# A gated linear-attention and GEGLU kernel: a new written order, a new split of work among the engines, and state products over whole 128-column tiles

## The chip, the cores and the metric

The kernel runs on one core of a Trainium2 chip. The core has five engines, each with a queue that it works off in order: TensorE (PE, matrix products; its weight loads are shown apart as PEld), VectorE (DVE), ScalarE (ACT), GpSimd (POOL) and SyncE (SP, which here only issues DMAs). POOL issues DMAs too. PE writes to PSUM, which DVE and ACT read; the other tiles are in SBUF.

The metric is the time of one execution on the device in microseconds. Before the change the median of three runs is 279.8 us (279.54 to 279.91).

## The reference

What is computed is a recurrence with a complex decay per step, followed by a gated feed-forward layer on its output (4 batches, 8 heads, 768 steps, 48 wide; 3072 tokens of 384 in the second part):

```python
mag = np.sqrt(a_re * a_re + a_im * a_im)
scale = np.minimum(mag, 0.999) / (mag + 1e-06)
a_re_n, a_im_n = (a_re * scale, a_im * scale)
for t in range(S):
    new_re = ar * S_re - ai * S_im
    new_im = ar * S_im + ai * S_re
    S_re, S_im = (new_re + kv, new_im)
    y[:, :, t] = np.einsum('bhd,bhde->bhe', q[:, :, t], S_re)
...
g = x @ w_gate
gelu = 0.5 * g * (1.0 + erf(g * inv_sqrt2))
ffn_out = gelu * (x @ w_val) @ w_out
res_gate = 1.0 / (1.0 + np.exp(-(x @ w_res)))
return x + res_gate * ffn_out
```

## The kernel before

**Tiles.** The sequence of a batch is cut into three stretches of 256 steps, each of two chunks of 128. A pair p = 4s + b is stretch s of batch b, so there are twelve pairs, 0 to 11, and the names of steps carry it: `QR6` is a step of pair 6, `X6.1` one of its second chunk, `AT6.1.0` one of the first four heads of that chunk. The feed-forward layer runs in seven units: pair 0, pair 1, then 2 and 3, 4 and 5, 6 and 7, 8 and 9, 10 and 11. `GP3.0` is a step of unit 3.

**The chain of one pair.** Loads `Lar`, `Lai`, `Lk`, `Lq`, `Lvf` on SP, 192 KB each. The gates: squares `SQI`, `SQR` (ACT or DVE), their capped sum `ADD` (DVE), `LNR` and `EXR` (ACT, 1/|re|), the tangent `TH` (DVE), `LM` (ACT, log magnitude), `ATN` (ACT, phase), running sums over the chunk by a product with a triangular matrix, `CSL` for the magnitude and `CST` for the phase (PE, fp32), `EX` and `EI` (ACT, the exponential and its inverse), then `OFF`, `FR`, `ABS` (reduction of the phase), `SIN` and `COS` (ACT). Products: `KE`, `QE` scale k and q, and `KR`, `QR` turn them into `padK` and `padQ`, 96 of 128 columns wide, the other 32 being zero (DVE). Attention within the chunk: for pairs 0 to 4 `TP` and `CP` transpose through PE and copy back, from pair 5 on `QT` and `KT` are transposing DMAs on SP; then `AT` (PE), `AM` (mask, DVE), `Y` (PE), `X` (copy to bf16, ACT or DVE).

**What is carried on.** `DK` (PE, line 612) adds up the state of a chunk, `MI` and `ED` take it over (DVE). Between stretches the state is decayed by `EN` (line 619) with a factor that `MM` and `MN` multiply together (lines 472 and 475) from small values that go through DRAM (`DR`, `DS`, `DE`, `DI`, `DT` on POOL), and copied to bf16 by `EB`. The phase is carried from chunk to chunk by `CRA` and `CRB` (line 533), which scale the last rows of the phase tile, and a DMA `CDA` or `CDB` (POOL, line 538), which adds the last of them to the next chunk's first row ahead of its `CST`.

**A unit.** `XT` and `XC` transpose x through PE for pairs 0 to 4, `XD` by DMA from pair 5 on; `GP` and `VP` are the gate and value products (PE), twelve steps of 512 columns each (six double steps in the units of one pair, so that GP0.0 to GP0.5 are all), `GE` the gelu (ACT), `HM` its product with the value (DVE), `RP` and `SG` the residual gate (PE, ACT), `OP` the output product (PE), `OT` its gating (DVE), `RX` the addition of x (POOL or DVE, line 729), `ST` the store (SP). Weights come by POOL's DMAs `Wg`, `Wv`, `Wr`, `Wo`; `HOLDW` and `HOLDO` are one-element copies on POOL that wait for a load of a_im and so hold back the weight loads written behind them.

**What sets the order.** `ORDER` is one list of step names, worked off from front to back under a manual schedule; each engine gets its instructions in that order, and waits between engines follow from the data and from tiles that are used again. The words `log`, `trig` and `gelu` in it load one of three function tables on ACT. `PARAMS['eo']` names the engine of single steps; `on(name, default)` looks it up. The PSUM tiles of the sums, the gate and value products and the transposes share four banks.

Of the kernel before, what the change touches and what calls it, by code (L numbers as in the profile page):

```python
# [64 lines left out]
 'eo': {'CP0.0.0.0': 'DVE',  # L65
        'CP0.0.1.0': 'DVE',
        'CP0.1.0.0': 'DVE',
        'CP0.1.1.1': 'ACT',
        'CP1.0.0.1': 'ACT',
        'CP1.1.0.0': 'DVE',  # L70
        'CP1.1.0.1': 'ACT',
        'CP1.1.1.0': 'DVE',
        'CP2.0.1.0': 'DVE',
        'CP3.0.0.1': 'ACT',
        'CP3.0.1.0': 'DVE',
        'CP3.0.1.1': 'ACT',
# [749 lines left out]
```

## Time and profile before

| | us |
|---|---|
| median of three runs | 279.8 |
| the profiled execution's span | 277.7 |
| PE busy | 239.6 (86%) |
| DVE busy | 225.6 (81%) |
| ACT busy | 199.7 (72%) |
| POOL busy | 82.6 (30%) |
| ACT table loads | 21, 26.9 in all |

The busy time of an engine is the time in which at least one of its instructions runs; neighbouring instructions of one engine overlap at their ends, so a busy engine is not always a full one. The granted TensorE clock is a share of full speed. DMA engines moved 41.33 MB, 149 GB/s over the span. 163,200 packets of them came from SP's queue, 7,488 from POOL's.

### The profile page before, as it was taken

To read this page: it belongs to the slowest core of one execution; us is meant where nothing else is said; L and a number is where in the kernel's file an instruction comes from. 1 tells how busy PE (TensorE), PEld (TensorE's weight loads), DVE (VectorE), ACT (ScalarE), POOL (GpSimd) and SP (SyncE) were. 2 spreads that over 40 slices of the span, in tenths; PEclk is the share of its full clock that TensorE was granted. 3 is DMA by queue.
4 is the path that set the end of the run, shared out by engine and by line. 5 is a ranking of instruction groups with operands and counts; after the bars stand their busy time and mean duration, and the time that the engine had idled before them with its cause. 6 is when DMAs were issued, how large, how long until landed. Compare 5 with 4: busy or idle time off the path is not lost.

```text
span 277.7 us, 5218 instructions
## 1 busy us (share of the span) xinstructions
PE 239.6 (86%) x1854; PEld 145.5 (52%) x1854; DVE 225.6 (81%) x390; ACT 199.7 (72%) x346; POOL 82.6 (30%) x127
## 2 busy tenths in 40 slices
PE   0446477977999978999999999999999999999993
PEld 0114345754687654546755466555566445654451
DVE  1369866698899999899999999999979999743533
ACT  5558867799989988999978889894776834415410
POOL 4013160320360464242546522600717400010001
PEclk9999955999899997999999999999999999999999
DMA  7999999999980499859969996889995794221003
GB/s 147 205 192 187 191 184 184 183 183 207 205 169 0 74 195 176 148 67 223 193 131 207 191 204 148 133 175 211 163 189 138 137 221 87 62 74 56 0 0 113
DMA packets 170712, 41.33 MB, mean 149 GB/s; under 512 B 162624, under 2 KB 170688, under 8 KB 170688
## 3 DMA queue, kind: packets, MB, share of 16 engines
q1 hardware_dynamic: 163200, 37.04, 67.3%
q0 software_dynamic: 7488, 3.97, 11.5%
q8 instruction: 14, 0.23, 0.3%
q14 instruction: 10, 0.08, 0.1%
HBM read 31.33 MB, written 4.76 MB: 130 GB/s over the span
## 4 chain that ended last, share of the span: by engine, by line
PE 54%; ACT 15%; DVE 12%; issue 8%; DMA 7%; POOL 2%; SPq 0%; DVEq 0%; POOLq 0%; ACTq 0%
PE gv L692 23%; PE sums L717 13%; ACT ar L370 4%; PE sums L455 4%; PE sums L488 4%; DVE h L703 3%; PE sums L707 3%; PE at L604 2%; ACT m L370 2%; DMA QT<-padQ 2%; ACT CS L370 2%; DMA KT<-padK 2%; DVE atm L607 1%; ACT Ei L370 1%; ACT L793 1%
## 5 line engine op out<-in xcount | busy, mean ns | idle before, releaser
L370 ACT ACTIVATE h<-gv 128x512 bf16<-128x512 f32 x72 | 41.5, 598 | 29.2 <-PE gv L692 28.3
L703 DVE SCALAR_TENSOR_TENSOR h<-h,gv 128x512 bf16<-128x512 bf16 x72 | 47.0, 681 | 14.0 <-PE gv L692 13.7
L692 PE MATMUL gv<-xT,wg 128*128 128x512 bf16 (+1 forms) x252 | 55.9, 359 | 1.8 <-ACT xT L377 1.5
L692 PE MATMUL gv<-xT,wv 128*128 128x512 bf16 (+1 forms) x252 | 55.0, 356 | 0.6 <-DVE h L703 0.6
L717 PE MATMUL sums<-wo,h 128*128 128x384 bf16 x288 | 50.5, 330 | 0.0
L717 PEld LDWEIGHTS <-h 128*128 128x128 bf16 x288 | 27.8, 99 | 18.3 <-issue 1.7
L692 PEld LDWEIGHTS <-wg 128*128 128x128 bf16 x252 | 24.9, 101 | 22.6 <-issue 3.4
L692 PEld LDWEIGHTS <-wv 128*128 128x128 bf16 x252 | 24.7, 100 | 21.4 <-issue 1.6
L607 DVE TENSOR_TENSOR atm<-at,mask 128x512 bf16<-128x512 f32 x48 | 31.7, 682 | 3.9 <-PE at L604 3.6
L793 ACT ACT_TABLE_LOAD x21 | 26.9, 1283 | 1.1 <-PEq L810 0.7
L370 ACT ACTIVATE ar<-ar 128x768 f32<-128x768 f32 (+1 forms) x31 | 25.6, 841 | 1.1 <-DVE m L431 1.0
L729 POOL TENSOR_TENSOR ot<-ot,x 128x384 f32<-128x384 f32 x13 | 15.2, 1189 | 32.4 <-DVE ot L722 32.3
L722 DVE SCALAR_TENSOR_TENSOR ot<-sg,sums 128x384 f32<-128x384 f32 x24 | 13.2, 549 | 10.4 <-PE sums L717 10.0
L378 POOL CAST v<-vf 128x384 bf16<-128x384 f32 x14 | 8.6, 619 | 42.4 <-DMA vf<-in_v_dram 42.4
L443 POOL DMA_DIRECT2D m<-d x16 | 11.3, 705 | 33.5 <-DVE M L475 23.2
L455 PE MATMUL sums<-m,lt 128*128 128x384 f32 x24 | 11.9, 583 | 10.5 <-DVE lt L286 8.7
L538 POOL DMA_DIRECT2D ai<-G x16 | 13.1, 820 | 24.3 <-ACT ai L370 13.9
L488 PE MATMUL sums<-ai,ut 128*128 128x384 f32 x40 | 17.8, 545 | 2.2 <-issue 1.0
L370 ACT ACTIVATE sg<-sums 128x384 f32<-128x384 f32 x24 | 11.6, 493 | 9.5 <-PE sums L707 9.4
L707 PE MATMUL sums<-wr,xT 128*128 128x384 bf16 x72 | 15.7, 332 | 0.0
L651 PE MATMUL y<-v,atm 128*128 128x48 bf16 x192 | 13.2, 187 | 2.7 <-DVE atm L607 2.7
L469 POOL DMA_DIRECT2D m<-d x16 | 13.8, 897 | 5.3 <-DMA d<-Ei 5.3
(89 smaller groups left out, 451.2 us busy)
## 6 DMA issues: line engine op xcount, KB each, us to landing
ai<-in_a_im_dram SPq DMA_DIRECT2D x24, 192.0 KB, 3.8
ar<-in_a_re_dram SPq DMA_DIRECT2D x24, 192.0 KB, 3.9
k<-in_k_dram SPq DMA_DIRECT2D x24, 192.0 KB, 3.9
q<-in_q_dram SPq DMA_DIRECT2D x24, 192.0 KB, 4.4
vf<-in_v_dram SPq DMA_DIRECT2D x24, 192.0 KB, 4.1
out_dram<-ot SPq DMA_DIRECT2D x24, 192.0 KB, 2.5
wg<-in_moe_w_gate_dram POOLq DMA_DIRECT2D x4, 288.0 KB, 8.1
wv<-in_moe_w_val_dram POOLq DMA_DIRECT2D x4, 288.0 KB, 9.0
```

Of the source, the lines that this page charges most:

```text
L370: return nc.scalar.activation(out=out, in_=in_, func=func, **kw)
L455: st.add("CSL%d.%d" % (p, c), "PE", lambda c=c: nc.tensor.matmul(out=st["csl", (p, c)], lhsT=lmat[c], rhs=part(("m2", p), (c,)), start=Tru ...
L469: st.add("DT%d.%d" % (p, u), "POOL", lambda u=u: nc.gpsimd.dma_start(out=st["m3", p][u * D:(u + 1) * D].rearrange("p r h -> p (r h)"), in_ ...
L488: return r + [nc.tensor.matmul(out=o, lhsT=tmat[c if s == 0 else 1], rhs=part(("ai", p), (c,)), start=not both, stop=True)]
L607: st.add("AM" + sfx, "DVE", lambda: nc.vector.tensor_tensor(out=st["atm", i], in0=st["at", i], in1=mask4, op=OP.mult), r=[("at", i)], w=[( ...
L651: r.append(nc.tensor.matmul(out=ys, lhsT=st["atm", (p, c, hg)][:, j], rhs=st["v", p][:, c, h], start=True, stop=first))
L692: st.add("%sP%d.%d" % (nm.upper(), u, f), "PE", lambda f=f, fs=fs, nm=nm, w=w: [nc.tensor.matmul(out=st[nm + "p", (u, f)][:, j * 256:j * 2 ...
L703: st.add("HM%d.%d" % (u, f), "DVE", lambda f=f, h2=h2: nc.vector.scalar_tensor_tensor(out=h2(), in0=h2(), scalar=0.5, in1=gv(("vp", (u, f) ...
L707: st.add("RP%d.%d" % (u, jj), "PE", lambda jj=jj: [nc.tensor.matmul(out=st["rp", (u, jj)], lhsT=st["xT", u][:, i, jj * 128:(jj + 1) * 128] ...
L717: st.add("OP%d.%d.%d" % (u, jj, hh), "PE", lambda jj=jj, fs=fs: [nc.tensor.matmul(out=st["op", (u, jj)], lhsT=st["h2", u][:, f, jj * 128:( ...
L729: st.add("RX%d.%d" % (u, jj), rese, lambda jj=jj, pc=(p, c), eng=eng: eng.tensor_tensor(out=st["ot", (u, jj)], in0=st["ot", (u, jj)], in1= ...
L793: nc.scalar.preload_act_table_set(tables[nm])
```

## The change

The order is written anew for all engines, and more steps can be given to POOL: the row scaling `CRA`/`CRB`, the products `MM`, `MN` and `EN` now look up their engine in `eo`. In numbers of steps, before to after:

| step | before | after |
|---|---|---|
| CRA, CRB | 16 DVE | 5 DVE, 11 POOL |
| EN | 8 DVE | 1 DVE, 7 POOL |
| MM and MN | 16 DVE | 8 DVE, 8 POOL |
| EB | 4 ACT, 4 DVE | 3 ACT, 2 DVE, 3 POOL |
| RX | 11 DVE, 13 POOL | 7 DVE, 17 POOL |
| VC (v to bf16) | 9 ACT, 1 DVE, 14 POOL | 7 ACT, 2 DVE, 15 POOL |
| SQI and SQR | 19 ACT, 7 DVE | 13 ACT, 13 DVE |
| CP | 18 ACT, 22 DVE | 16 ACT, 24 DVE |
| X | 17 ACT, 7 DVE | 15 ACT, 9 DVE |
| table loads | 21 | 31 |

The code that changes, and one stretch of the order, the one around the last pairs' gates and the first half of unit 4:

```diff
+    def engine(e):
+        return nc.gpsimd if e == "POOL" else nc.vector
...
-            st.add("MM%d" % p, "DVE", lambda: nc.vector.tensor_tensor(
+            mme, mne = on("MM%d" % p, "DVE"), on("MN%d" % p, "DVE")
+            st.add("MM%d" % p, mme, lambda: engine(mme).tensor_tensor(
...
-            st.add("MN%d" % p, "DVE", lambda: nc.vector.tensor_tensor(
+            st.add("MN%d" % p, mne, lambda: engine(mne).tensor_tensor(
...
-        cre = PARAMS["cre"]
-        eng = nc.gpsimd if cre == "POOL" else nc.vector
+        cre = on("CR%s%d" % (nm, p), PARAMS["cre"])
+        eng = engine(cre)
...
-            return [nc.tensor.matmul(out=d[0:DD, h * D:(h + 1) * D], lhsT=K(c * H + h), rhs=st["v", p][:, c, h],
+            return [nc.tensor.matmul(out=d[:, h * D:(h + 1) * D], lhsT=st["padK", p][:, c * H + h], rhs=st["v", p][:, c, h],
...
-            st.add("EN%d" % p, "DVE", lambda: nc.vector.tensor_tensor(
+            ene = on("EN%d" % p, "DVE")
+            st.add("EN%d" % p, ene, lambda: engine(ene).tensor_tensor(
...
-OT3.3 GP4.0 Lq10.0 MM9 gelu OT3.2 GP4.1 KR8 Lvf9.1 GP4.2 GE4.0 VP4.0 RX3.2 GE4.1 QE8 GP4.3 GE4.2 RP4.1 KT8 HM4.0 GE4.3
-GP4.4 QR8 SG4.1 RP4.0 GE4.4 RX3.3 GP4.5 SG4.0 MM8 ED7 GP4.6 GE4.5 MN8 QE9 VP4.1 QT8 GE4.6 VP4.2 HM4.1 RP4.2 HM4.2
...
+CST9.1 Lvf8.0 COS8 OFF9.1 Y7.1 TH10 OT3.0 ATN11 X7.1 FR9.1 ATN10 DK7.1 OP3.1.0 OP3.2.0 XD7.1 Lk9.0 ABS9 MM8 MN8 OT3.3
+QE8 QR8 OT3.2 SIN9 COS9 GP4.4 gelu GE4.4 DT9.1 RX3.0 KE8 KR8 GP4.2 GE4.2 ST3.0 GP4.11 GE4.11 CDB7 GP4.5 VC8.0 DT9.0
+GP4.10 OT3.1 GP4.1 KE9 ED7 GE4.10 GE4.5 VP4.5 VP4.1 KR9 GE4.1 CSL10.0 log EX10.0 HM4.5 HM4.1 DS10.0 CDB6 EI10.0 ME9
```

With the wider state product, PE writes all 128 rows of the state tile; rows 96 to 127 come from the zero columns of `padK` and are not read.

The start of the order, up to the first transposes of pair 0 (before, then after, each cut short):

```
Lai0.0 log Lar0.0 Lar0.1 Lai0.1 SQI0.0 Lk0.0 LNR0.0 SQR0.0 EXR0.0 Lar1.0 ADD0.0 LNR0.1 LM0.0 Lar1.1 SQR0.1 CSL0.0
SQI0.1 Lai1.0 ADD0.1 LM0.1 EXR0.1 Lk0.1 CSL0.1 TH0.1 TH0.0 Lai1.1 EI0.1 Lq0.0 EX0.0 EX0.1 EI0.0 Lar2.0 KE0.0 trig SQR1
...
Lar0.0 log LNR0.0 SQR0.0 Lar0.1 Lai0.1 Lai0.0 LNR0.1 SQR0.1 EXR0.1 SQI0.1 SQI0.0 ADD0.1 LM0.1 TH0.1 EXR0.0 ADD0.0
Lai1.0 Lai1.1 Lar1.1 Lar1.0 LM0.0 CSL0.0 CSL0.1 TH0.0 trig ATN0.1 ATN0.0 SQR1 SQI1 Lai2.0 Lai3.0 ADD1 CST0.1 CST0.0
OFF0.1 FR0.1 ABS0.1 OFF0.0 log EI0.0 EX0.0 EX0.1 LNR1 EXR1 FR0.0 TH1 Lvf0.0 LM1 ABS0.0 trig COS0.0 SIN0.0 ATN1 SIN0.1
Lar2.1 Lar2.0 Lai2.1 VC0.0 SQR2 SQI2 Lk0.0 KE0.0 ADD2 Lar3.1 Lar3.0 COS0.1 SQR3 Lk0.1 Lai3.1 DE0 CSL1.1 CSL1.0 SQI3
```

The new order as a whole has the tables in the sequence log trig log trig log trig, then from GP0 on gelu log gelu log trig, from GP1 on gelu log trig, from GP2 on gelu log trig log trig, from GP3 on gelu log trig, from GP4 on gelu log gelu log gelu trig, from GP5 on gelu log gelu. Before, it was log trig log trig gelu ahead of GP0, log trig up to GP1, gelu log trig for each unit up to GP5, then gelu gelu.

The first products of a unit are no longer its lowest-numbered ones: units 1 to 6 start at GP1.5, GP2.10, GP3.11, GP4.4, GP5.3 and GP6.6.

## The prediction

> **What bounds the kernel now.** I read the profiled execution by stages. A stage ends where the first gate product of the next feed-forward unit starts on PE (lines GP0 to GP6 of the written order, found in the timeline at 43.6, 74.7, 106.5, 146.2, 182.1, 217.4 and 247.7 us). This is the view of busy time by windows; its columns are the window, its length, then PE, PEld, DVE, ACT, POOL busy us (instructions), the granted clock, the DMA share and GB/s.
>
> ```profile
> 0.00:43.62 43.62, 18.59 (x111) 11.07 (x112) 27.60 (x52) 30.28 (x50) 12.46 (x28) 0.89 1.04 184
> 43.62:74.71 31.09, 27.13 (x213) 19.02 (x212) 24.23 (x41) 26.75 (x42) 6.33 (x11) 0.88 1.13 192
> 74.71:106.46 31.75, 28.87 (x310) 22.25 (x309) 31.43 (x56) 29.38 (x54) 14.62 (x22) 0.99 0.62 118
> 106.46:146.15 39.69, 38.98 (x312) 22.88 (x311) 37.14 (x65) 35.31 (x65) 16.21 (x24) 0.97 0.84 157
> 146.15:182.06 35.91, 35.77 (x281) 20.72 (x279) 34.68 (x60) 31.12 (x55) 16.14 (x23) 1.00 0.94 177
> 182.06:217.37 35.31, 35.05 (x264) 19.91 (x263) 32.51 (x57) 25.43 (x47) 12.93 (x18) 1.00 0.88 169
> 217.37:247.68 30.31, 29.72 (x244) 16.87 (x245) 25.12 (x44) 12.73 (x23) 2.11 (x3) 1.00 0.59 119
> 247.68:277.70 30.02, 25.46 (x134) 12.82 (x131) 12.92 (x21) 8.69 (x16) 1.77 (x2) 0.98 0.13 46
> ```
>
> From 106 us on PE is busy nearly throughout; in the first two stages no engine is, and the DMA engines run full. Busy times overlap at their ends, so for sums I take the pitch, the start-to-start distance of instructions that follow at once. The chain of waits (start, us, what) gives two of them:
>
> ```profile
> 249.63 14.24 PE gv L692 x66
> ...
> 265.34 7.81 PE sums L717 x48
> ```
>
> 14.24/66 is 216 ns for a 512-column product, 7.81/48 is 163 ns for a 384-column one, against 384 and 330 ns of "busy". In the same way from the timeline: GP or VP step 0.65 us, OP 1.95, RP 0.49, CSL or CST 0.65 to 0.70, TP 0.45, Y 0.41 (16 products), DK 0.34 (8 products); on DVE 0.87 for 768 fp32 columns, 0.47 for 384, 0.60 for HM or AM; on ACT 0.73, 0.37 and 0.49 (GE). Summed over the steps of each stage, before and after (DK still at its old price, as are the moved steps at their new engine's nearest row):
>
> | stage | took | PE, DVE, ACT before | PE, DVE, ACT after |
> |---|---|---|---|
> | 0 | 43.6 | 9.7, 26.1, 29.9 | 12.3, 26.7, 32.8 |
> | 1 | 31.1 | 22.3, 22.9, 23.4 | 19.7, 24.2, 22.5 |
> | 2 | 31.8 | 27.3, 30.0, 29.5 | 26.8, 28.0, 28.5 |
> | 3 | 39.7 | 36.9, 34.1, 34.1 | 37.3, 36.8, 35.2 |
> | 4 | 35.9 | 35.2, 33.1, 29.3 | 35.2, 32.0, 28.5 |
> | 5 | 35.3 | 34.5, 30.4, 23.0 | 34.5, 29.8, 25.4 |
> | 6 | 30.3 | 29.4, 23.3, 11.6 | 29.4, 18.7, 13.9 |
> | 7 | 30.0 | 25.3, 11.4, 7.5 | 25.3, 11.4, 7.5 |
>
> So stages 4 to 6 lose under 1 us each to waits and can hardly be ordered better. Stage 7 is products plus a fixed drain. Stages 0 and 1 lose 13.7 and 7.7 us beyond their fullest engine. What a new order can win lies there.
>
> **The parts, one by one.** The rows of the view of groups by form that price them (line, engine, operation, shapes, count, busy us, mean ns, idle before):
>
> ```profile
> L793 ACT ACT_TABLE_LOAD x21 | 26.9, 1283 | 1.1 <-PEq L810 0.7
> ...
> L729 POOL TENSOR_TENSOR ot<-ot,x 128x384 f32<-128x384 f32 x13 | 15.2, 1189 | 32.4 <-DVE ot L722 32.3
> ...
> L651 PEld LDWEIGHTS <-atm 128*128 128x128 bf16 x192 | 11.8, 98 | 6.1 <-DVE atm L607 3.2 <-issue 0.9
> ...
> L612 PEld LDWEIGHTS <-padK 128*96 128x96 bf16 x160 | 10.1, 132 | 3.1 <-DVE Gb L378 1.3 <-issue 0.6
> ...
> L378 POOL CAST v<-vf 128x384 bf16<-128x384 f32 x14 | 8.6, 619 | 42.4 <-DMA vf<-in_v_dram 42.4
> ...
> L533 DVE TENSOR_SCALAR G<-m 32x384 f32<-32x384 f32 x16 | 6.7, 416 | 0.5
> ...
> L619 DVE TENSOR_TENSOR G<-G,M 96x384 f32<-96x384 f32 x8 | 4.4, 547 | 0.0
> ```
>
> *State products.* A 96-column weight load takes 132 ns, a 128-column one 98 ns. DK's eight products follow at 43 ns each (93.01 to 93.35 us in the timeline), Y's sixteen, with 128-column loads among 96-row ones, at 25 ns (86.83 to 87.24). If DK falls to Y's pitch, a step saves 8 x 18 ns = 0.144 us. Twelve of the 20 steps lie in stages 3 to 6, where PE is what ends: -1.7 us; the eight others are covered by ACT and DVE. Bounds: 0 (the load was not the limit) and -2.9 (all 20 count).
>
> *Moves between engines.* DVE gives up 11 row scalings CR at 0.39 pitch, 7 decays EN at 0.47, net 4 residual adds RX at 0.47, 8 small M products at 0.08 and 2 copies EB at 0.27, and takes six more squares at up to 0.87, two CP, two X, one VC: 211.3 to 207.4 us in all. ACT loses the squares but loads ten more tables at 1.29 pitch (31 for 21): 188.4 to 194.3. POOL's price for CR and EN is in no row. For EN the bounds are 0.55 (DVE's row) and 1.19 (POOL's two-input row, 128 partitions), for CR 0.42 and 1.19; I take 1.19 and 0.5, the cast's row of 0.62 being the nearest one-input one. EN then costs up to 0.64 us more between the last decay product and Y. That is covered by other products where EN is written early, as it is except at EB4 and Y4.0 (1.3 us short).
>
> The trace holds a cost of POOL work that its own rows hide. This is the timeline around 148 to 151 us (start, us, engine, line):
>
> ```profile
> 147.71 1.72 POOL L729 TENSOR_TENSOR ot<-ot,x 128x384 f32<-128x384 f32 x1
> 150.01 0.93 POOL L729 TENSOR_TENSOR ot<-ot,x 128x384 f32<-128x384 f32 x1
> ```
> ```profile
> 149.65 2.11 DVE L558 TENSOR_TENSOR padQ<-CS,qE 128x1536 bf16<-128x1536 bf16 x1
> ```
>
> The rotation takes 0.95 us elsewhere; here it took 1.16 more, beside a POOL add of 0.93. Six DVE operations with both inputs in SBUF (QE3, QE10, KR4, KR10, QR6, ADD5) ran 0.24 to 1.16 us long, 3.65 us in all, each over a POOL add or cast, while HM and AM, which read PSUM, never did. POOL's adds and casts are 24.1 us now and some 46 after (17 RX, 15 VC, 11 CR, 7 EN, 3 EB, 8 small ones at the prices above), so by the same share DVE loses 7.0, 3.4 more than now: its relief of 3.9 us is gone. I count this inside stages 1 to 3 only; later PE covers it. The Trainium skill speaks against this part ("SBUF — State Buffer", section "Who interferes with whom"): GpSimd's ports are VectorE's second pair, taken as a lock for a whole instruction, and a VectorE instruction with two SBUF inputs waits for a GpSimd one that reads SBUF. By that rule every such meeting costs up to a whole instruction, as QR6 shows; the rows show it at six of the 78 operations KE, QE, KR, QR, TH and ADD.
>
> *The new order, stage 0.* ACT must do 23.3 us before TP0.0.0 (13.8 before the change), starting at 3.6 when the first load is in: 26.9 at best. q of pair 0 is now the 20th and 21st load; at 192 KB and 184 GB/s a load takes 1.07 us, so 3.6 + 20 x 1.07 = 25.0, and up to 3.2 later because Wg0 and Wr (576 KB) are now ahead of the hold step on POOL's queue. TP0.0.0 then starts at 27 to 29.5, against 23.4. But behind it there is less: ACT 9.5 and DVE 8.9 us up to GP0.0, against 16.2 and 15.9, which took 20.1. Walked step by step (CP 0.6, TH3 0.95, FR1, QR0.1, two AM, TH2, X0.0, MI0, two AM, Y0.1, X0.1, XT, XC) it is some 11 us. GP0.0 at 40.0, from 36.4 (ACT without a gap) to 43.6 (no gain): -3.6 us, with 2.6 us more PE work done by then, of which stage 1 is relieved.
>
> *Stages 1 and 2.* The fullest engines sum to 53.4 now and 52.7 after, in 62.9 us. POOL work stands against it: -0.5, bounds -5.5 and +5.
>
> *Stage 3.* PE 36.7 with faster DK; DVE 2.7 fuller, and two more table loads. +1.5, bounds 0 and +9.
>
> *Stages 4 to 6.* I compared how much PE work is written between a producer and the product that needs it. For the phase carry (CR, then a DMA of 3.4 us, then CST) the order leaves 2.0, 1.7, 1.4 and 2.1 us uncovered at CST5.1, 6.1, 7.1 and 9.1, 7.2 in all; before 5.2, of which the trace shows 1.9 as gaps on PE. By that share +0.7. For the transposing DMA ahead of GP4 to GP6 it left 1.4 to 1.7 uncovered and leaves none now; the trace shows one gap of 0.45: -0.4.
>
> Sum: -1.7 - 3.6 - 0.5 + 1.5 + 0.7 - 0.4 = -4.0. The profiled span is 277.7, the median of the runs 279.8, 2.1 more; 277.7 - 4.0 + 2.1 = **275.8**.
>
> **Rivals.** *Stage 3 jams* (slower). Between GP2 and GP3 ACT now loads gelu, log, trig, log, trig, where it was gelu, log, trig; DVE, ACT and PE are within 2 us of each other, so a late GE, HM or decay stops the others. If the stage runs at stage 1's ratio, 31.1/23.4 = 1.33, it takes 36.8 x 1.33 = 48.9, +9.2 for the +1.5 above: 275.8 + 7.7 = 283.5. It decides from a ratio of 1.23, where it eats the 5.5 us of the rest. For it: that ratio of stage 1, and the DVE stalls. Against it: stage 2 was just as level (27.3, 30.0, 29.5) and took 1.06 of its fullest.
>
> *POOL work holds DVE up* (no change). DVE waits at a POOL operation as at QR6 and passes the wait on to PE: in stages 1 to 3 some 20 POOL operations are new; 3.65 us over the 27 present ones is 0.14 each, and 0.2 with EN's longer reads, so 4 us: 279.8. For it: the six long operations. Against it: 72 others of their kind without it. It is the lock of the Trainium skill's page above, at work in this kernel.
>
> *Stage 1 tightens too.* At stage 2's ratio 24.2 x 1.06 = 25.7 for 31.1: 5.4 less, 270.4. For it: gates of pairs 2 and 3 are now done before GP0. Against it: four table loads inside it.
>
> That the wider tile doesn't load faster costs the 1.7 alone: 277.5, inside the forecast.
>
> **How the numbers follow.** Forecast (272 to 279.2) 0.43, jam 0.32, hold-up 0.12, tighter stage 1 0.13. A measurement of this kernel tells 0.2%, 0.56 us, from no change. Faster: 0.43 + 0.13 + a sixth of the hold-up's = 0.58; same, about half of the hold-up's: 0.07; slower 0.35. Range 269 to 286: below it a tighter stage 1 with all bounds of stage 0 good, above it a jam beyond 1.40. The forecast's own is 272 to 279.2.
>
> **What would show it.** LDWEIGHTS of padK near 98 ns and DK at 25 ns; GP0.0 at 40 us, GP2's first product at 102.4, GP3's at 143.6; the last stage at 30.0; DVE rotations longer than 1.4 us in twice as many places; 31 table loads. It is wrong if GP0.0 is later than 43.6, or if PE has gaps beyond 5 us between GP2 and GP3.

## The result, and the profile after

The changed kernel takes 291.3 us (median of four runs, 289.4 to 293.0); before, run beside it, takes 279.7. The ratio is 1.042 [1.035, 1.049]: slower by 11.6 us, where the prediction had 275.8 and a range of 269 to 286. Medians here and below are over all executions, the ratios leave out those more than 1.5% above the fastest of the same kernel. The profiled execution's span is 288.1 us, 10.4 more than before; its stages (units start at 45.1, 77.42, 109.44, 150.39, 190.17, 229.06 and 258.46 us) in the view of busy time by windows:

```profile
0.00:45.10 45.10, 19.59 (x119) 10.73 (x120) 29.93 (x56) 34.61 (x56) 15.69 (x31) 0.81 1.07 183
45.10:77.42 32.32, 23.23 (x204) 16.68 (x204) 23.40 (x40) 23.42 (x35) 7.47 (x10) 0.89 0.87 152
77.42:109.44 32.02, 27.59 (x306) 20.79 (x307) 28.69 (x52) 28.80 (x53) 19.44 (x25) 1.00 0.97 170
109.44:150.39 40.95, 38.49 (x315) 21.99 (x315) 39.35 (x62) 36.99 (x63) 25.31 (x32) 1.00 0.74 146
150.39:190.17 39.78, 36.89 (x276) 20.46 (x277) 37.16 (x56) 30.41 (x53) 24.37 (x33) 0.96 0.80 155
190.17:229.06 38.89, 35.09 (x263) 19.39 (x260) 34.15 (x53) 28.06 (x47) 18.42 (x25) 1.00 0.74 147
229.06:258.46 29.40, 29.26 (x244) 16.77 (x245) 20.23 (x35) 14.12 (x26) 3.66 (x5) 1.00 0.54 113
258.46:288.10 29.64, 25.46 (x134) 12.83 (x131) 12.67 (x21) 8.91 (x16) 3.46 (x4) 1.00 0.15 54
```

Against the prediction's boundaries, the span of 273.7 that it stood for came out 14.4 longer: stage 0 by 5.1 (45.1 for 40.0), stages 1 and 2 together by 1.9 (64.3 for 62.4), stage 3 by nothing (40.95 for 41.2), stages 4 to 6 by 8.0 (108.1 for 100.1), the last one by -0.4. In stages 4 and 5 PE is busy for 36.9 and 35.1 us, before for 35.8 and 35.1; it stands still for 2.9 and 3.8, where it stood still for 0.1 and 0.3.

The prices, from the groups by form (line, engine, operation, shapes, count, busy us, mean ns, idle before):

```profile
L949 ACT ACT_TABLE_LOAD x31 | 39.8, 1283 | 1.3 <-PEq L966 0.7
...
L688 POOL TENSOR_SCALAR G<-m 32x384 f32<-32x384 f32 x11 | 15.4, 1403 | 30.4 <-DVE m L657 24.0 <-issue 5.5 <-POOL G L775 0.4
...
L775 POOL TENSOR_TENSOR G<-G,M 96x384 f32<-96x384 f32 x7 | 8.6, 1222 | 18.5 <-DVE M L630 18.4
...
L767 PEld LDWEIGHTS <-padK 128*128 128x128 bf16 x160 | 6.5, 98 | 2.8 <-issue 1.1 <-DVE Gb L794 0.6
L627 POOL TENSOR_TENSOR M<-m 96x8 f32<-96x8 f32 x5 | 3.3, 656 | 3.0 <-DMA m<-d 2.9
```

The wider state product loads its weights in 98 ns (132 before), as foretold. A decay EN on POOL takes 1222 ns for my 1.19 us; but a row scaling CR takes 1403 ns, where I had put 0.5, and DVE needed 416.

Now the front. POOL's timeline (start, us, line, out<-in, [idle before <-releaser]) shows which transfers are let go and when:

```profile
14.97 0.81 POOL L920 DMA_DIRECT2D wg<-in_moe_w_gate_dram  x1
15.78 0.76 POOL L923 DMA_DIRECT2D wr<-in_moe_w_res_dram  x1
16.54 0.63 POOL L912 COPY HOLDW<-ai 1x1 f32<-1x1 f32 x1
17.11 0.77 POOL L920 DMA_DIRECT2D wg<-in_moe_w_gate_dram  x1
30.42 0.45 POOL L912 COPY HOLDO<-ai 1x1 f32<-1x1 f32 x1 [12.54 <-DMA ai<-in_a_im_dram]
30.82 1.52 POOL L920 DMA_DIRECT2D wg<-in_moe_w_gate_dram  x2
```

Wg0, Wr and Wg2 go at 15.0 to 17.9 us, nine more weight transfers from 30.8 to 40.1. The two loads that the chain of waits (start, us, what) then names are SP's:

```profile
18.03 8.77 DMA ai<-in_a_im_dram
26.89 0.97 DVE m L556
...
33.84 19.10 DMA k<-in_k_dram
53.06 0.96 DVE kE L705
54.44 0.97 DVE padK L713
```

The first is Lai3.1: it takes 8.8 us against a median of 3.9 for its kind (5.6 in a later run, e11, which holds the weights back), and SQI3 starts only at 26.9; ADD3, LM3 and CSL3.1 hang on it, and TP0.0.0 starts at 32.5. The second is Lk1.0, 19.1 us after its issue, with the nine weight transfers beside it. The summary of waits from 20 to 58 us (who, waited for whom: us, times, longest) gives what each costs:

```profile
PEld sums L609 <- ACT m L521: 9.9, 1, 9.9
...
DVE kE L705 <- DMA k<-in_k_dram: 6.6, 1, 6.6
PE tp L745 <- DVE padK L713: 6.5, 1, 6.5
```

The 9.9 us are the weight load of CSL3.1, which waits for LM3. DVE's 6.6 us are spent standing at KE1, and PE's 6.5 are the same wait one step on: KR1, TP1, DK1.0.

Then stage 4. Here are DVE, POOL and PE in one stretch of the timeline:

```profile
158.16 1.66 DVE L705 TENSOR_TENSOR qE<-q,E 128x768 bf16<-128x768 f32 x1
159.85 1.55 DVE L713 TENSOR_TENSOR padQ<-CS,qE 128x1536 bf16<-128x1536 bf16 x1
161.44 1.55 DVE L705 TENSOR_TENSOR kE<-k,Ei 128x768 bf16<-128x768 f32 x1
163.02 1.14 DVE L713 TENSOR_TENSOR padK<-CS,kE 128x1536 bf16<-128x1536 bf16 x1
164.08 0.67 DVE L859 SCALAR_TENSOR_TENSOR h<-h,gv 128x512 bf16<-128x512 bf16 x1
```
```profile
158.96 1.54 POOL L775 TENSOR_TENSOR G<-G,M 96x384 f32<-96x384 f32 x1
160.47 1.69 POOL L885 TENSOR_TENSOR ot<-ot,x 128x384 f32<-128x384 f32 x1
162.12 1.22 POOL L532 CAST Gb<-G 96x384 bf16<-96x384 f32 x1
```
```profile
164.81 0.65 PE L863 MATMUL sums<-wr,xT 128*128 128x384 bf16 x3 [2.89 <-DVE h L859]
```

QE7, QR7 and KE7 each run some 0.6 us beyond their 0.95, under EN7, an RX and EB7. HM3.3 is written behind all four key and query steps, so it ends at 164.75, and PE, which waits 2.9 us for the PSUM banks that it holds, starts RP3.1 at 164.81. Two effects meet here, POOL's and the written order's; the runs take them apart. The wait also costs something behind it. The granted clock is 1.00 up to it, 0.73 from 164.8 to 167 us, 0.50 to 169 and 0.95 to 171, and PE is busy 1.1 us longer in this stage than before.

In stage 5 PE's longest wait follows from one long operation. From the timelines of DVE and POOL, and the summary of waits of PE from 109 to 230 us:

```profile
190.69 2.49 DVE L713 TENSOR_TENSOR padQ<-CS,qE 128x1536 bf16<-128x1536 bf16 x1
193.11 0.54 DVE L878 SCALAR_TENSOR_TENSOR ot<-sg,sums 128x384 f32<-128x384 f32 x1
```
```profile
190.94 1.42 POOL L775 TENSOR_TENSOR G<-G,M 96x384 f32<-96x384 f32 x1
```
```profile
PE gv L848 <- DVE ot L878: 2.1, 1, 2.1
```

QR8 takes 2.49 us in place of 0.95, beside EN8 on POOL. OT3.2 stands behind it on DVE, and GP4.11 on PE starts when OT3.2 has ended, at 193.7 us.

### The profile page after: what moved, and what is told of

Read it like the earlier page. It is cut to its first block, busy times and chain, and to the rows that moved or that the text cites. A ratio compares the mean times of both kernels' runs of the same rounds, so it can differ in the third digit from the quotient of the medians.

```text
span 288.1 us, 5184 instructions
## 1 busy us (share of the span) xinstructions
PE 235.6 (82%) x1854; PEld 139.6 (48%) x1854; DVE 225.6 (78%) x369; ACT 205.3 (71%) x343; POOL 117.8 (41%) x161
## 4 chain that ended last, share of the span: by engine, by line
PE 36%; DVE 17%; DMA 16%; ACT 11%; issue 9%; SPq 7%; POOL 4%; DVEq 0%; POOLq 0%; ACTq 0%
PE gv L848 20%; DMA k<-in_k_dram 7%; SPq L537 6%; PE sums L873 5%; DMA m<-d 4%; ACT L949 3%; DMA ai<-in_a_im_dram 3%; DVE h L859 2%; PE sums L609 2%; PE sums L863 2%; DMA xT<-x 2%; DVE qE L705 2%; PE sums L643 2%; PE at L759 2%; ACT CS L521 2%
## 5 line engine op out<-in xcount | busy, mean ns | idle before, releaser
L859 DVE SCALAR_TENSOR_TENSOR h<-h,gv 128x512 bf16<-128x512 bf16 x72 | 47.2, 680 | 14.7 <-PE gv L848 13.8
L848 PE MATMUL gv<-xT,wv 128*128 128x512 bf16 (+1 forms) x252 | 56.7, 360 | 0.2 <-DVE h L859 0.2
L848 PE MATMUL gv<-xT,wg 128*128 128x512 bf16 (+1 forms) x252 | 52.2, 348 | 5.4 <-DVE ot L878 2.1
L873 PE MATMUL sums<-wo,h 128*128 128x384 bf16 x288 | 49.4, 326 | 0.0
L949 ACT ACT_TABLE_LOAD x31 | 39.8, 1283 | 1.3 <-PEq L966 0.7
L885 POOL TENSOR_TENSOR ot<-ot,x 128x384 f32<-128x384 f32 x17 | 18.6, 1098 | 40.3 <-DVE ot L878 40.2
L688 POOL TENSOR_SCALAR G<-m 32x384 f32<-32x384 f32 x11 | 15.4, 1403 | 30.4 <-DVE m L657 24.0
L521 ACT ACTIVATE ar<-ar 128x768 f32<-128x768 f32 (+1 forms) x28 | 22.9, 831 | 0.1
L609 PE MATMUL sums<-m,ut 128*128 128x384 f32 x24 | 12.5, 615 | 11.6 <-ACT m L521 11.6
L521 ACT ACTIVATE sg<-sums 128x384 f32<-128x384 f32 x24 | 11.6, 492 | 11.6 <-PE sums L863 10.0
L521 ACT ACTIVATE m<-m 96x8 f32<-96x8 f32 (+2 forms) x29 | 13.5, 469 | 8.1 <-DVE m L585 4.5
L531 ACT COPY qk<-tp 96x512 bf16<-96x512 bf16 x16 | 9.0, 580 | 12.5 <-PE tp L745 6.8
L705 DVE TENSOR_TENSOR kE<-k,Ei 128x768 bf16<-128x768 f32 (+1 forms) x13 | 12.4, 958 | 6.7 <-DMA k<-in_k_dram 6.6
```

Source lines behind the costliest of these rows:

```text
L521: return nc.scalar.activation(out=out, in_=in_, func=func, **kw)
L609: st.add("CSL%d.%d" % (p, c), "PE", lambda c=c: nc.tensor.matmul(out=st["csl", (p, c)], lhsT=lmat[c], rhs=part(("m2", p), (c,)), start=Tru ...
L705: st.add(nm.upper() + "E%d%s" % (p, sfx), "DVE", lambda cs=cs, nm=nm, E=E: nc.vector.tensor_tensor(out=part((nm + "E", p), cs), in0=part(( ...
L848: st.add("%sP%d.%d" % (nm.upper(), u, f), "PE", lambda f=f, fs=fs, nm=nm, w=w: [nc.tensor.matmul(out=st[nm + "p", (u, f)][:, j * 256:j * 2 ...
L859: st.add("HM%d.%d" % (u, f), "DVE", lambda f=f, h2=h2: nc.vector.scalar_tensor_tensor(out=h2(), in0=h2(), scalar=0.5, in1=gv(("vp", (u, f) ...
L873: st.add("OP%d.%d.%d" % (u, jj, hh), "PE", lambda jj=jj, fs=fs: [nc.tensor.matmul(out=st["op", (u, jj)], lhsT=st["h2", u][:, f, jj * 128:( ...
```

## The experiments

| run | us | ratio to before [95%] |
|---|---|---|
| changed kernel | 291.3 | 1.042 [1.035, 1.049] |
| e3 weights held | 286.1 | 1.021 [1.017, 1.026] |
| e2 POOL's five kinds back | 288.1 | 1.029 [1.024, 1.035] |
| e4 both | 282.6 | 1.009 [1.006, 1.012] |
| e11 both, HM early | 280.9 | 1.005 [1.002, 1.008] |
| e1 before + wide products | 279.0 | 0.997 [0.994, 1.000] |
| e8 (the same program) | 278.9 | 0.994 [0.991, 0.997] |
| e7 e1 + POOL's five kinds | 281.1 | 1.001 [0.998, 1.005] |
| e5 new front, old back | 278.8 | 0.995 [0.992, 0.997] |
| e6 old front, new back | 287.3 | 1.026 [1.022, 1.031] |
| e9 e6 with old engines | 301.1 | 1.071 [1.064, 1.078] |
| e10 e1 + six loads | 287.6 | 1.023 [1.015, 1.031] |
| e15 e1 + six plain steps | 284.2 | 1.018 [1.013, 1.023] |
| e12 e1, DVE relieved | 280.1 | 1.002 [0.999, 1.005] |
| e13 e11, five loads fewer | 291.5 | 1.043 [1.039, 1.048] |
| e14 e11, seven loads fewer | 304.4 | 1.088 [1.084, 1.092] |
| e16 e1, DVE and ACT swapped | 285.3 | 1.017 [1.013, 1.021] |
| e17 e11, DVE relieved | 290.4 | 1.034 [1.029, 1.039] |
| e18 e5, DVE relieved | 280.0 | 0.999 [0.996, 1.002] |

"Front" is all that is written up to unit 2, "back" the rest; POOL's five kinds are CR, EN, EB, MM and MN. Stage lengths in us from the profiles of the main ones:

| | 0 | 1 | 2 | 3 | 4 | 5 | 6 |
|---|---|---|---|---|---|---|---|
| before | 43.6 | 31.1 | 31.8 | 39.7 | 35.9 | 35.3 | 30.3 |
| e1 | 43.0 | 30.4 | 32.1 | 38.5 | 36.3 | 35.4 | 30.0 |
| e8, e1 again | 43.0 | 31.2 | 32.8 | 39.0 | 35.9 | 36.8 | 29.6 |
| changed | 45.1 | 32.3 | 32.0 | 40.9 | 39.8 | 38.9 | 29.4 |
| e3 | 42.9 | 27.5 | 35.3 | 42.2 | 40.5 | 38.6 | 29.4 |
| e2 | 44.7 | 31.4 | 32.0 | 44.0 | 38.2 | 36.3 | 29.5 |
| e4 | 42.6 | 26.2 | 31.3 | 43.8 | 40.6 | 35.8 | 29.5 |
| e11 | 43.1 | 25.1 | 32.0 | 44.2 | 39.2 | 35.9 | 29.5 |
| e5 | 42.6 | 26.4 | 31.3 | 42.2 | 36.3 | 35.3 | 30.4 |
| e6 | 43.3 | 31.6 | 33.8 | 43.7 | 38.6 | 38.0 | 29.5 |

e1 and e8 are one program, profiled in executions of 277.9 and 280.5 us, and their stages differ by up to 1.4 us; less than that is not read from this table.

### The wide products alone (e1), and a repeat of it (e8)

```diff
-            return [nc.tensor.matmul(out=d[0:DD, h * D:(h + 1) * D], lhsT=K(c * H + h), rhs=st["v", p][:, c, h],
+            return [nc.tensor.matmul(out=d[:, h * D:(h + 1) * D], lhsT=st["padK", p][:, c * H + h], rhs=st["v", p][:, c, h],
```

> The order and the engines of before, with the state products alone over 128 columns. Theory: the 96-column weight load was the limit of DK, so DK falls from 43 to some 25 ns a product and the time by 1 to 3 us (ratio 0.990 to 0.997). Rival: the load was hidden, DK keeps its pitch and the time is the same within 0.5 us. A second rival: the wide tile costs, and is part of why the change is slower: over 280.5 us.

```profile
L615 PEld LDWEIGHTS <-padK 128*128 128x128 bf16 x160 | 6.7, 99 | 4.5 <-issue 1.9 <-DVE Gb L380 1.5
```

In the old order the load falls from 132 to 99 ns, and the span from 277.7 to 275.8. Run against before the gain is 0.9 us, with an interval that just reaches 1.

In e8 each of six words that load a table was written twice:

```diff
-log
+log log
```

> The old order with the wide state products and with six table loads doubled behind unit 2's start (log and trig twice each in stages 3 to 5), which is 7.8 us more of ACT, as many as the new order has more there. Theory E (the extra table loads are what stages 3 to 5 lose): 5 to 8 us over 279.0. Rival (ACT has room: 34, 29 and 23 us of work in stages of 38 to 35): under 2.5 us more.

Its profile has 21 loads: two loads without a use between them became one. So it says nothing of loads. As a repeat of e1 it gives 278.9 us and a gain of 1.7 us, with an interval clear of 1; the wide products are worth 0.9 to 1.7 us.

### The weights held back (e3), POOL's steps on DVE (e2), both (e4)

e3 writes Wg0 behind HOLDW, Wr and Wg2 behind HOLDO, the output weights behind a new hold on a_re of pair 5, and Lk1 earlier:

```diff
- 'holds': {'HOLDW': ('ai', 2, 1), 'HOLDO': ('ai', 4, 1)},
+ 'holds': {'HOLDW': ('ai', 2, 1), 'HOLDO': ('ai', 4, 1), 'HOLDX': ('ar', 5, 1)},
...
-TH3 Wg0 Wr CP0.0.1.0 FR1.0 AT0.0.0 CSL3.0 CP0.0.1.1 EX1.0 Lq1.0 ... HOLDW ... Wg2 ... HOLDO Lk1.1 Lk1.0 AM0.1.0 Wg1 Wg3
+TH3 CP0.0.1.0 FR1.0 AT0.0.0 CSL3.0 CP0.0.1.1 EX1.0 Lk1.1 Lk1.0 Lq1.0 ... HOLDW Wg0 ... HOLDO AM0.1.0 Wg1 Wr Wg2 Wg3
...
+Wv3 HOLDX Wo0 Wo2 Wo1
```

> The changed kernel with its weight loads behind holds as before the change (Wg0 after HOLDW, Wr and Wg2 after HOLDO, Wo after a third hold on the load of pair 5's a_re) and k of pair 1 loaded two places earlier. Theory C (loads of a and k wait behind weights on the DMA engines, which keeps DVE and ACT idle in the first 55 us): GP0.0 falls from 45.1 to 39 to 42 us, the 6.9 us gap of PE at DK1.0 is gone, and the time falls by 4 to 8 us. Rival: something else in stage 0 and 1 takes the place of the loads, GP1's first product stays within 1.5 us of 77.4 and the time is the same within 2 us.

e2 changes 29 engines:

```diff
-        'CRA4': 'POOL',
-        'CRA5': 'POOL',
+        'CRA4': 'DVE',
+        'CRA5': 'DVE',
...
```

> The changed kernel with CR, EN, EB, MM and MN back on DVE where they had gone to POOL; order, RX, VC and squares as changed. Theory A (POOL's long row scalings and decays hold up the carry chain, and DVE waits beside them): stages 3 to 5 lose most of their 8.7 us, so 291.3 falls by 4 to 8 us, to 283 to 287, and the stretched DVE operations (17 now) fall under 10. Theory B (the new order itself, whatever the engines): the same as changed within 2 us.

> Both edits, the holds and the five steps back on DVE. If theories A and C hold and are in different stages, their gains add: 278 to 282 us. If only the order counts, over 287.

e3 gives back 5.2 us. Its first stages:

```profile
0.00:42.90 42.90, 20.31 (x119) 11.69 (x120) 28.43 (x53) 34.80 (x56) 12.67 (x28) 0.84 1.21 181
42.90:70.40 27.50, 24.23 (x205) 16.84 (x205) 24.69 (x42) 23.62 (x35) 9.98 (x14) 0.88 1.08 177
```

Stage 1 takes 27.5 us for 32.3 with no less work on any engine, and the wait of DVE for k is gone: KE1 starts at 46.7 us (43.9 in e11, which holds the weights in the same way), in the changed kernel at 53.1. e3 changes two things at once, the holds and the place of Lk1; how much each gives is not told apart.

The five kinds on DVE give 3.2 us (e2), and 3.5 on top of e3. In the profiles of e3 and e4 the gain lies in stages 2 and 5 (4.0 and 2.8 us), in those of the changed kernel and e2 in stages 4 and 5 (1.6 and 2.6). Stage 3 goes the other way: 43.8 us for 42.2, and 44.0 for 40.9. Long DVE operations (over 0.15 us beyond the usual length of their form) fall from 16 to 10 in e2, and from 8.8 to 5.6 us in all; under 10 had been expected. How much of the gain is DVE's waiting beside POOL, and how much POOL's own slower row scalings and decays in the carry, the runs don't separate.

### HM early (e11)

```diff
-QE7 QR7 GE3.1 VP3.3 VP3.11 KE7 Lk9.1 GP3.7 KR7 HM3.3 QT6 RP3.0 ... CDB4 HM3.11 CDB5
+QE7 QR7 GE3.1 VP3.3 HM3.3 VP3.11 HM3.11 KE7 Lk9.1 GP3.7 KR7 QT6 RP3.0 ... CDB4 CDB5
```

> The changed kernel with the weights held back and GpSimd's five kinds on VectorE (282.6 us), with two steps moved in the written order: HM3.3 straight behind VP3.3, HM3.11 straight behind VP3.11, ahead of the key steps of phase 7 that were written between. Theory 1, the product of gate and value that is written late holds its PSUM banks and so TensorE: the 2.7 us gap between RP3.0 and RP3.1 goes, and 2 to 2.7 us of the time with it (280 to 280.7). Theory 2, VectorE has no room in stage 4, so that the wait turns up behind the next key step: the gap moves, and the time changes by less than 0.7 us.

PE's timeline of e11 at the same place:

```profile
155.31 1.39 PE L862 MATMUL sums<-wr,xT 128*128 128x384 bf16 x6
156.54 0.61 PE L758 MATMUL at<-QT,KT 96*128 96x128 bf16 x8
```

RP3.0 and RP3.1 now follow at once (six products in one row). In e4, with the five kinds on DVE, the wait was still 2.6 us, so most of it is the written order's. Behind them a wait of 0.9 us is new, at Y6.0, whose masks DVE does later; none of the old size turns up. The granted clock is 1.00 throughout stage 4, where in e4 it fell to 0.81 and 0.50 in the four microseconds behind the wait. By the medians 1.7 us come back, by the ratios 0.9, with intervals that overlap: the gap and its cause are shown, its worth is between the two.

### Where the rest is lost: the front (e5) or the back (e6), and POOL in the old order (e7)

e5 is e4's order up to GP2.10 and the order and engines of before from there; e6 is e1's up to GP2.0 and e4's from there. Both lists were joined and the table words put ahead of their first use.

> The new order up to the first product of unit 2, with the weight loads held and the five kinds of steps on DVE as in the run with both edits; from there on the old order and its engines; state products over 128 columns. Theory D (the new order gains in stages 0 to 2 once its loads are mended, and loses in stages 3 to 6): unit 2 starts at 100 to 102 us, the rest takes the 170 us that it takes in the old order, 270 to 272 of span and 272 to 274 us. Rival (the front only borrows from what follows, by leaving steps of pairs 4 to 7 undone): unit 2 starts at 101, the rest takes 175 or more, over 276.

> The old order and engines up to the first product of unit 2, the new order from there on, with CR, EN, EB, MM and MN on DVE; state products over 128 columns. Theory D: the part behind unit 2's start takes 177 to 180 us as in the two runs with the steps back on DVE (170 in the old order), so 284 to 288 us. Rival (the new back suffers only from what the new front hands it): 170 to 173, 278 to 281 us.

The new front with the weights held brings unit 2 forward by 5.2 us (100.3 against 105.5) and loses 3.7 of them in stage 3. ACT and PE of e5 at the boundary:

```profile
103.12 0.84 ACT L519 ACTIVATE ai<-ai 128x768 f32<-128x768 f32 x1 [2.17 <-DVE ai L564]
103.98 1.28 ACT L947 ACT_TABLE_LOAD   x1
105.28 0.49 ACT L519 ACTIVATE sg<-sums 128x384 f32<-128x384 f32 x1
```
```profile
105.82 2.10 PE L846 MATMUL gv<-xT,wg 128*128 128x512 bf16 x9 [3.41 <-ACT sg L519]
```

Unit 2 has begun, but ACT still owes ATN6, which waits 2.2 us for TH6 on DVE; the gelu table and the first SG come behind it, and PE waits 3.4 us. PE was brought forward, the other queues were not.

The new back on the old front loses 8.3 us against e1 with POOL's five kinds on DVE: stages 3, 4 and 5 grow by 5.2, 2.3 and 2.6 (in profiled executions that lie 12 us apart, so the shares count, not the sum). PE's gaps between 105 and 230 us, counted as starts later than the pitch allows, are 16.9 us against 3.8 in e1, in many places and none over 2.5.

e7 gives e1's order the changed kernel's engines for POOL's five kinds:

```diff
+        'CRA4': 'POOL',
...
+        'EN6': 'POOL',
...
```

> The old order with the wide state products and with those of CR, EN, EB, MM and MN on POOL that the change puts there. Theory A (these moves cost in any order: POOL takes 1.4 us for a row scaling and 1.2 for a decay, and DVE waits beside them): 3 to 6 us over the 279.0 of the wide products alone, and stretched DVE operations rise from 9 to some 17. Rival (they cost only where the order gives POOL's queue no time): within 1.5 us of 279.0.

By the medians 2.0 us more than e1, by the ratios 1.1, with intervals that overlap: the same moves cost the old order less than the 3.2 to 3.5 that they cost the new one. The long DVE operations did not rise to 17 as expected: 11, 6.0 us in all, for 8 and 4.6 in e1.

### Is it the table loads? (e10, e15, e13, e14)

e10 adds at six places behind GP2.0 a load and a one-element step that uses it; e15 puts four small squares there in place of both.

```diff
-gelu
+log ZL2 gelu
```
```diff
-gelu
+ZZ2 gelu
```

> Before with wide state products, and six more table loads, each with a one-element ScalarE operation behind it that keeps the load from being dropped, spread from unit 2 on: 27 table loads and six operations more. A load takes 1.28 us. The changed kernel makes 31 loads where before makes 21. Theory 1, ScalarE's loads sit on the chain that feeds the next product: 6 x 1.3 us = 7.7 us more ScalarE time, of which most is lost: 284 to 287 us against 279.0. Theory 2, ScalarE has room from unit 2 on: within 2.5 us of 279.0, and the loads are no large part of what the new order loses.

> Before with wide state products (279.0 us, 21 loads), and at the six places where table loads were added in an earlier run four small ScalarE squares (128x216, an estimated 0.36 us each, from 0.51 for 384 and 0.84 for 768 columns) in place of the load and its one-element operation: 1.45 us more ScalarE work at each of the six, no load more. Theory 1, at the places where ScalarE goes from one table to the next it is what the others wait for, whatever it does: 285 to 289 us, as with the six loads. Theory 2, only a table load costs so much (it also empties ScalarE and holds its queue): 279 to 282 us.

Six loads cost e1 8.6 us (7.3 by the ratios) for 8.9 us more of ACT (six times 1.283 and 0.202): nearly all is paid, though ACT is free for 76 us of e1 (199.3 busy in 275.8). The plain steps, 24 of 0.384 us, cost 5.2 (5.9 by the ratios); the intervals of the two runs overlap, so a load's price is not told apart from that of any other ACT time at the same places. They stand at the changes from one table to the next, where, as I read it, ACT has finished one kind of step and the next kind is waited for.

So the new order's six more loads behind unit 2 looked like the missing 8 us. e13 and e14 take loads out of e11:

```diff
-GP2.8 OT1.0 gelu GE2.8 ... MI4 log LM6 trig ATN6 VP2.0
+GP2.8 OT1.0 TH6 ATN6 gelu GE2.8 ... MI4 log LM6 VP2.0
...
-log ML10 X8.0 ME10 ... EX11.1 DT11.1 EI11.1 ... MM10 gelu SG4.1 ... X8.1 SG4.0 OFF11.1 ... OT4.1 RX4.1 MN10 trig COS10
+X8.0 ... DT11.1 ... MM10 SG4.1 ... X8.1 SG4.0 log ML10 ME10 EX11.1 EI11.1 OFF11.1 ... OT4.1 RX4.1 MN10 DS11.1 ML11 ME11 trig COS10
```

> The kernel with the weights held, GpSimd's five kinds on VectorE and HM early (280.9 us, 31 table loads), with five loads taken out by moving a few steps in the written order: ATN6 to the other arctangents ahead of unit 2 (TH6 with it), ME9 behind EXR10, the pair EX11.1, EI11.1 and ML10, ME10 behind SG4.0, ML11 and ME11 ahead of COS10 (DS11.1 with them). 26 loads. Theory 1, as six more loads cost the old order 8.7 us, each load of the new order is paid in full: 5 x 1.3 = 6.4 us less, 274 to 276 us. Theory 2, the new order leaves its loads in places where ScalarE waits anyway: 279.5 to 281.5 us. Theory 3, the moved steps come too late for what reads them: over 281.5.

> As the run before, and the two log groups of stage 4 joined: the sums CSL10.0, CSL11.0, CSL10.1, CSL11.1 of phases 10 and 11, their exponentials and what hangs on them come behind all of unit 4's GE and SG. 24 loads in place of 31. Theory 1, loads paid in full: 7 x 1.3 = 9 us under 280.9, 271 to 273.5 us, stage 4 at 36 us (39.2 before). Theory 2, loads covered: 279.5 to 281.5. Theory 3, phases 10 and 11 come too late with their exponentials: stage 5 grows by over 2 us, and the time stays above the run before.

Both are far slower. In e13, stages 2 and 3, where two loads went with ATN6, take 76.2 us, as in e11: those two were covered, or what they freed was lost again. Of the 10.6 us, 8.4 are lost in stage 5 (44.3 for 35.9), at one place that the edit itself made. ACT's timeline of e13:

```profile
215.68 0.57 ACT L520 ACTIVATE m<-sums,magic 128x384 f32<-128x384 f32 x1
221.88 0.45 ACT L520 ACTIVATE m<-m 96x8 f32<-96x8 f32 x2 [5.63 <-issue]
222.34 1.28 ACT L948 ACT_TABLE_LOAD   x1
223.64 0.93 ACT L520 ACTIVATE CS<-ai,hpi 128x768 bf16<-128x768 f32 x1
```

and PE's:

```profile
229.44 0.58 PE L847 MATMUL gv<-xT,wg 128*128 128x512 bf16 x1 [8.50 <-DMA xT<-x]
```

ML11 reads what the transfer DS11.1 brings. POOL issues it at 219.42, behind RX4.1, which can start only when OT4.1 has ended on DVE (217.8). With ML11 ahead of COS10, COS10 runs at 223.6 in place of 213.7, and X9.1, which is written behind it on ACT, makes the transposes of unit 5 late. In e14 it is stage 5 again, 57.8 us for 35.9: PE waits 2.7 and 5.3 us for the phase carries of pairs 10 and 11, which come late, and 6.1 for the transposes. The new order's last pair of loads (log, gelu, around ML11) is the price of not standing there. So it is not borne out that the loads explain the back's loss. It isn't ruled out either: they were taken out in these two ways only, and both brought new waits.

### Is it the load of DVE? (e12, e17, e18)

```diff
-        'OFF6.0': 'DVE',
-        'X6.0': 'DVE',
+        'OFF6.0': 'ACT',
+        'X6.0': 'ACT',
...
```

> Before with wide state products (279.0 us), order unchanged, with ten steps of stages 3 to 5 moved from VectorE to ScalarE: the offsets of six phases (OFF5.1 to OFF10.1) and X6.0, X7.1, X8.1, X10.1, together 4.7 us of VectorE. Theory 1, VectorE bounds stages 3 to 5 (it is free for 1.5 to 2.3 us in each): 275 to 277.5 us. Theory 2, TensorE bounds these stages, as the prediction took it: within 0.7 us of 279.0.

> The kernel with the weights held, GpSimd's five kinds on VectorE and HM early (280.9 us), order unchanged, with five steps that the change gave to VectorE back on ScalarE: SQR8, SQI9, SQR11, X5.1, X7.0 (3 us of VectorE in stages 3 and 4; ScalarE is free for some 7 us of stage 3 and 9 of stage 4 by the busy columns). Theory 1, stage 3 is VectorE's (42.0 us busy in 44.2): 277.5 to 279 us and stage 3 at 41 to 42.5. Theory 2, what holds stage 3 is where ScalarE's steps stand in its queue, and five more make it worse: 281 to 285 us.

> The kernel with the new front (held weights) and the old order and engines behind unit 2 (278.8 us; stage 3 takes 42.2 us, against 38.5 without the new front), with the same ten offsets and X steps on ScalarE that gained nothing in the old order (e12). Theory 1, the front's 5 us are lost again in stage 3 because VectorE is behind by then: relieved of 4.7 us it keeps 2 to 3.5 us of them: 275.3 to 277 us, stage 3 at 39 to 40.5. Theory 2, they are lost to something else (ScalarE, loads of data): 278 to 280 us.

(One of e12's ten steps, OFF5.1, is on ACT in e5 already, so that e18 moves nine.) In none of the three does the relief gain: it changes nothing in the old order, loses 9.5 us in the new one and 1.2 in e5 (there with intervals that just overlap). In e17 half of the loss is one step. ACT's timeline, then PE's:

```profile
108.27 0.61 ACT L520 ACTIVATE h<-gv 128x512 bf16<-128x512 f32 x1
113.11 0.84 ACT L520 ACTIVATE m<-ai 128x768 f32<-128x768 f32 x1 [4.23 <-issue]
113.86 0.47 ACT L520 ACTIVATE sg<-sums 128x384 f32<-128x384 f32 x1
```
```profile
114.38 1.86 PE L847 MATMUL gv<-xT,wg 128*128 128x512 bf16 x4 [4.65 <-ACT sg L520]
```

The step at 113.11 is SQI9. Its output is one of four tiles that the pairs use in turn, and the last reader of pair 5's is CRB5 on DVE, which ends at 113.0. On DVE, SQI9 is written straight behind CRB5 and waits for nothing (112.4 us in e11). The profile names no releaser for the wait; the times fit CRB5. On ACT SQI9 stands 4.2 us with SG2.0, GE2.11 and GE2.2 behind it, and PE waits for the banks that these free.

### Do order and engines belong together? (e9, e16)

e9 is e6's order with each step on the engine of before; e16 is e1's order with the 58 squares, copies, offsets and X steps swapped between DVE and ACT as the change has them.

```diff
-        'SQR8': 'DVE',
+        'SQR8': 'ACT',
...
```
```diff
+        'SQR8': 'DVE',
...
-        'OFF6.0': 'DVE',
+        'OFF6.0': 'ACT',
...
```

> Written order of the changed kernel from GP2.0 on, written order of before ahead of it, every step on the engine that before gives it, wide state products. The same order with the changed kernel's squares, copies, offsets and X steps (but GpSimd's five kinds on VectorE) took 287.3 us, and the order of before with wide products 279.0. Theory 1, the steps that moved from ScalarE to VectorE load VectorE in stages 3 to 5: with them back on ScalarE, stage 3 falls from 43.7 to 39 to 40.5 us and the time to 280 to 283 us. Theory 2, the written order itself puts steps in the wrong place whoever does them: the time stays between 285 and 289 us, and TensorE's gaps between 105 and 230 us stay over 12 us (16.9 in the run before, 3.8 in the old order).

> Before with wide state products (279.0 us), order unchanged, and the 58 squares, copies, offsets and X steps that the change moves between ScalarE and VectorE moved as it moves them (some each way: net 14 more on VectorE, 9 fewer on ScalarE). GpSimd's steps as in before. Theory 1, an order fits the engines it was written for: as the new order lost 13.8 us with the old engines, the old order loses with the new ones: 284 to 290 us. Theory 2, the moves balance, and only VectorE's added time counts (estimated 3 us of squares): 279 to 282 us.

The new order loses 13.8 us more with the old engines, stage 3 taking 52.9 us for 43.7; the old order loses 6.2 us with the new ones. In e9 neither DVE nor ACT has more to do than in e6 in that stage (37.1 and 33.6 us by its windows; 40.1 and 33.9 in e6). What grows is waiting at the heads of queues. PE's two longest waits there are 2.7 us, where SQI9 is on ACT again with SG2.0 behind it, and 3.9 us at AT4.1.1, whose copy stands on ACT behind ML7, which waits for a transfer. The granted clock falls to half behind both, 0.92 in the mean of the stage.

## Why the prediction was wrong

*State products.* Right: 98 ns for the load, and DK's eight products at 25 ns a piece. The term was -1.7; alone it measured -0.9 and -1.7.

*The new order, stage 0.* The walk held as far as ADD2 (20.6 us). The step that failed is "up to 3.2 later because Wg0 and Wr (576 KB) are now ahead of the hold step on POOL's queue": I charged the weights to q of pair 0 only. Also behind them were a_re and a_im of pair 3 (24.1 and 26.9 us), and SQR3, SQI3, ADD3, LM3 and CSL3.1 are written ahead of TP0.0.0. And no term at all stood for the nine weight transfers that meet Lk1. Together they measured 5.2 us (e3, with Lk1 moved up), mostly in stage 1: of the 5.1 us of stage 0 only some 2 come back. With the weights held TP0.0.0 starts at 29.3 us (e11), inside my 27 to 29.5, and GP0.0 still at 43.1: from there to GP0.0 it took 13.8 us, not the 11 of the walk. The walk left out ABS1 and two of the copies on DVE (1.3 us), and 1.4 us in which DVE waits for AT0.1.1, behind copies that ACT does only after a table load and ATN3.

*Moves between engines.* For CR I wrote "I take 1.19 and 0.5, the cast's row of 0.62 being the nearest one-input one". It measured 1.40, above the upper bound of 1.19 as well, and with 0.66 for the small products POOL's compute came to 59 us in place of 46. The long DVE operations came as foretold in size but not in place. Of the six kinds that I had counted, 13 ran 6.9 us over their usual length, for my 7.0; of all kinds 16 ran 8.8 us over, of which 6.4 in stages 4 and 5, where I had written "later PE covers it". It doesn't: QR8 alone made PE wait 2.1 us, and the moves cost 3.2 to 3.5 us (e2, e4). The sign that I had put for it did not come: rotations over 1.4 us were three before (KR4, QR6, KR10) and three after (QR6, QR7, QR8). The page "SBUF — State Buffer" of the Trainium skill, section "Who interferes with whom", says that a VectorE instruction with two SBUF inputs contends with a GpSimd one that reads SBUF, for a pair of ports that is locked. QR8, 1.54 us longer beside a decay of 1.42, agrees in size; but of some 28 operations of my six kinds that ran beside a POOL computation, 15 kept their usual length.

*Stage 3.* 40.95 for 41.2, in part by luck. With POOL's five kinds back on DVE the stage takes 43.7 to 44.2 us, whether it starts at 100 us (e4, e11) or at 108 to 109 (e2, e6); with them on POOL 40.9 and 42.2 (e3). So the moves relieve this stage by 1.6 to 3.1 us, where I had written "its relief of 3.9 us is gone". What made up for that relief in the sum is not known.

*Stages 4 to 6.* The largest failed step, 8.0 us. "Stages 4 to 6 lose under 1 us each to waits and can hardly be ordered better" was true; from it I priced only two kinds of wait, the phase carry and the transposes (+0.3). They could be ordered worse, and no term stood for that, nor for the clock that falls behind a wait of PE: e11 still loses 2.9 us in stage 4 against e1, e6 2.3 and 2.6 in stages 4 and 5, and HM3.3, which was in no list of mine, 0.9 to 1.7.

*Table loads.* Ten more entered only as a sum of busy time and as "two more table loads" in stage 3. In the old order ACT's time at such places is paid nearly in full; two of the new order's were covered, and the rest is open.

*The rivals.* The jam of stage 3 was the wrong stage. The hold-up by POOL was there (QR8, OT3.2, GP4.11) and the moves cost 3.2 to 3.5 us for its 4, one of three losses and not the whole; but it stood in stages 4 and 5, not in 1 to 3. I had held the "72 others" against it that ran at their usual length: by the timelines of before only some six of them ran beside a POOL computation at all, so about half of those that did were long, as after the change. I had weighed them as alternatives; they came together with the weights, which no rival named.

So the three mended, weights 5.2, POOL's steps 3.5 and HM 1.7, are 10.4 of the 11.6 us, and e11 is still 1.9 us over e1, which has the wide products too. That rest is a difference of two larger things: a front that is 5.3 us earlier (unit 2 at 100.2 against 105.5) and a back that is 8.1 longer (178.4 against 170.3 to the end of the span). Which places make the back longer stays open. Shown is that the steps taken off DVE in e12, e17 and e18 don't mend it, and that an order and its division of work go together: each order with the other's engines lost 6 and 14 us. Left open are the loads (e13 and e14 brought waits of their own), whether DVE's load is what lengthens stage 3 (e17 brought a wait of its own too, and the five kinds on POOL do shorten that stage), and which of the single placements count.

No version beat before by much: e1 and e5, 278.8 to 279.0 us, are the fastest.

## What to carry to other kernels

In a kernel with in-order queues and three engines busy for 70 to 86% of the span, total busy time by stage says what can't be won, not what will be lost. For each step that is moved, ask three things: which loads and weight transfers are now issued beside the ones it waits for, which tile it writes and who reads that last, and what is queued behind it on its new engine while it waits. A gain at the front of one engine counts only if the others have no backlog there.

## What the runs showed of the hardware

- GpSimd needed 1403 ns to scale 32x384 fp32 by a column where VectorE needed 416, more than its own two-input add over 128x384 (1098); on 96x8 it took 656 against 156.
- A 192 KB load on SP's queue took 19.1 us to land with nine weight transfers of POOL's beside it, against a median of 4.1. The Trainium skill ("DMA: Bandwidth & Descriptors", section "Issuing engines are not separate DMA queues") says that transfers of all issuing engines run on the same sixteen DMA engines and interleave; the trace agrees: in e3, with the weights held and the load written earlier, it took 9.6 us.
- The Trainium skill's page "ScalarE: Activation LUTs", section "What ACT_TABLE_LOAD costs", puts a switch of tables at 1283 ns and 1380 ns more for draining. The load is 1283 ns here too, but nothing like the rest is seen: in e13 the load starts 0.02 us after the step ahead of it has ended (222.34) and the next step 0.01 us behind it (223.64), and six loads in e10, each with a small step, cost 8.6 us.
- Behind a wait of PE of some 2 us or more the granted clock mostly fell to half for about 4 us: after the 2.9 us at 164.8 us of the changed kernel, the 2.6 us in e4, the 4.65 us in e17. It did not after the 2.1 us at 193.7, nor after the 3.4 us in e5.
